# Starting four first-MLP sums of the first batch before their last third is there

## The chip, the cores and the metric

One core of a Trainium2 chip runs the whole program. The metric is device microseconds of one execution; the number given for a kernel is the median over its runs. Engines are called PE (TensorE matmul; PEld its weight loads), ACT (ScalarE), DVE (VectorE), POOL (GpSimd) and SP (SyncE, which issues most DMAs).

## What is computed

Attention with normalised queries and keys over 8 batches, 12 heads, 448 positions, 64 channels, and then one MLP over the 3584 tokens that come out:

```python
q_n, k_n = rmsnorm(q, g_q), rmsnorm(k, g_k)
attn = softmax(q_n @ k_n.T / 8)            # per batch and head
x = (attn @ v) -> (3584 tokens, 768)       # heads side by side
h = x @ w_in                               # 768 -> 2048
g = max(h, 0) + alpha * min(h, 0)          # alpha: one number per column
out = g @ w_out                            # 2048 -> 768
```

## The kernel before

**Tiles.** A batch's 12 heads are cut in three groups of four (G = 3), so there are 24 groups, numbered y = 3 b + i. A group has seven score tiles (y, j), one per 64 keys: `score` (L212) makes one with four matmuls (line 217) into one of two PSUM tiles `sc` of two banks each (pool `pss`, L55), and `soft` (L226) takes its exponential on ACT into `expT` (line 229). When all seven are there, `den` (L249) sums them over the keys with 28 matmuls against ones (line 240, tile `dn`), `log` and `invert` (L253, L258) turn that into 1/sum on ACT as exp(-ln), and `attv` (L262) makes the 28 matmuls with v (line 240, tile `av`) and lets DVE multiply both into the group's third of `xT[b]` (line 268). `dn`, `av`, the transposes `tps2` of groups 3 to 7, and some MLP tiles (`hTa`, `opa`) all use the one PSUM tile of pool `psa`, tag "acc" (two banks, one buffer); the other MLP tiles rotate through two banks of `psf`, tag "mm". Together they are eight banks.

**Before the scores**, each group's q and k are loaded (`load_qk`, SP's queue, six buffers `nat`), squared on POOL (`square`, line 135), summed on DVE (`reduce`, line 141), turned into factors by two small ACT steps (`root`, lines 152 and 153), scaled to fp16 (`scale`, line 158, on POOL but for a few on DVE), and transposed: groups 0 to 7 on PE with two DVE copies that give qT and kT (`turn`, lines 193, 202 and 204), the later ones by DMA (`turn_dma`) with a small DVE step (line 179).

**The MLP** of a batch: 16 units "up" (L279), each six matmuls 128x128 by 128x448 over the six thirds-by-two of `xT[b]` (line 284), then ACT's scaled copy `ah` (line 292) and DVE's maximum into `gT` (line 293); the sums over 768 need all three groups of the batch, the third last. And units "down" (L297): 16 matmuls over all of `gT` and `w_out_sb` (line 301) for 128 tokens and half of the columns, a DVE copy, and the store. Two batches give 14 of them. The weights come by POOL's DMA queue in four pieces each (`load_w_in`, `load_w_out`).

**Order.** Nothing reorders: each engine does its instructions as the program emits them. The program goes through 66 "bursts" n (L489). A burst emits two or three score tiles and their exponentials, and a `den` (in `dens`), an `attv` (in `avs`) or neither ("plain"); then a root and its scalings, then the MLP units planned for it, `gaps[n]`, among which the `turn` of a coming group stands. In a plain burst whose first unit is an up, the second exponential waits behind that unit's `ah` ("late", L518). The planner (L384 to L440) gives units costs of 1.13 and 2.6, cuts the run into periods that begin with the `attv` of a batch's third group, and fills each burst until a clock passes its share. `prep` and `post` hold loads, squares and reduces by burst; `jobs` holds reduces that follow the burst's units or go inside its first down. Two bursts are `lead` (L494): the `den` of group 2 (burst 11) and its `attv` (burst 12) go before the scores there, and in 11 eight and in 12 three matmuls on zeros (`spin`, L323) keep PE busy.

Of the kernel before, what the change touches and what calls it, by code (L numbers as in the profile page):

```python
# [9 lines left out]
FP32 = mybir.dt.float32  # L10
# [11 lines left out]
def kernel(  # L22
# [12 lines left out]
    nc = tc.nc  # L35

    B, H, S, D = q.shape
# [4 lines left out]
    G = HH // 2  # L42
# [188 lines left out]
            scale=QK_SCALE, bias=expb[:, 0:1],  # L231
        )

    def over_keys(name, y, weights):
        acc = psa.tile([128, 2, 512], FP32, name=name, tag="acc")
        e = expT[y]
        for j in range(J):
            for g in range(2):
                for par in range(2):
                    nc.tensor.matmul(  # L240
                        out=acc[ds(64 * par, 64), g, :S],
                        lhsT=weights(g, par, j),
                        rhs=e[ds(64 * g, 64), j, par, :],
                        start=(j == 0),
                        stop=(j == J - 1),
                    )
        return acc
# [11 lines left out]
        r = rden[y]  # L259
        nc.scalar.activation(out=r, in_=r, func=AF.Exp, scale=-1.0)  # L260

    def attv(y):  # L262
        b, i = divmod(y, G)
        vv = vt[b]
        av = over_keys("av", y, lambda g, par, j: vv[ds(64 * g, 64), 2 * i + par, j, :])
        if i == 0:
            xT[b] = att.tile([128, 2, G, S], FP16, name="xT", tag="xT")
        nc.vector.tensor_mul(  # L268
            out=xT[b][:, :, i, :], in0=av[:, :, :S], in1=rden[y]
        )  # L270


    def bank(name, spare):
        if spare:
            t = psa.tile([128, 2, 512], FP32, name=name + "a", tag="acc")
            return t[:, 0]
        return psf.tile([128, 512], FP32, name=name, tag="mm")

    def up(b, ft, spare=False):  # L279
        x = xT[b].rearrange("p g i c -> p (g i) c")  # L280
        hT = bank("hT", spare)
        order = [g * G + i for i in range(G) for g in range(2)]
        for c in order:
            nc.tensor.matmul(  # L284
                out=hT[:, :S],
                lhsT=w_in_sb[:, c, ts(ft, 128)],
                rhs=x[:, c, :],
                start=(c == order[0]),
                stop=(c == order[-1]),
            )  # L290
        ah = ffn.tile([128, S], FP16, name="ah", tag="ah", bufs=3)
        nc.scalar.activation(out=ah, in_=hT[:, :S], func=AF.Copy, scale=alpha_sb[:, ft : ft + 1])  # L292
        nc.vector.tensor_max(out=gT[:, ft, ds((b & 1) * S, S)], in0=hT[:, :S], in1=ah)  # L293
# [43 lines left out]
    while m < NG * J or len(avs) < NG:  # L337
        n = len(bursts)
        if len(dens) > len(avs):
            avs[n] = len(avs)  # L340
        elif len(dens) < NG and last_in.get(len(dens), n) < n:
            dens[n] = len(dens)
        three = n in dens and dens[n] >= G or n in avs and avs[n] >= G
        count = min(3 if three else 2, NG * J - m)
        bursts.append([divmod(m + c, J) for c in range(count)])
        for y, j in bursts[n]:
            first_in.setdefault(y, n)
            if j == J - 1:
                last_in[y] = n
        m += count  # L350
# [5 lines left out]
    def at(n, f, *a):  # L356
        prep.setdefault(max(int(n), 0), []).append((f, a))
# [4 lines left out]
    turn_at = {  # L362
        y: max(n for n in range(first_in[y]) if n not in dens) for y in range(1, NG)
    }
    turn_at[2] = av_at[0] + 1
    turns = {n: y for y, n in turn_at.items()}
    jobs = {}
    for y in range(G, NG):

        early = y < G + 2  # L370
        n = turn_at[y - 1] if early else max(d for d in dens if d <= turn_at[y] - 2)
        at(n - (8 if early else 5), load_qk, y)
        for nm in "qk":
            (after if early else at)(n - 2, square, y, nm)
            if early:
                after(n, reduce, y, nm)
            else:
                jobs.setdefault(n, []).append((reduce, (y, nm)))
        roots[n + 1] = y
    for b in range(1, B):  # L380
        at(av_at[G * b] - 4, load_v, b)


    UP, DOWN = 1.13, 2.6  # L384

    periods, carry = [], []
    for b in range(B):
        ups = [(UP, up, (b, ft)) for ft in range(NF)]
        odd = b % 2
        new = [  # L390
            (DOWN, down, (b - odd, t, oh))
            for t in (range(3, J) if odd else range(3)) for oh in range(2)
        ]
        tail = len(new) if b == B - 1 else 2 if odd or b == 0 else 1
        periods.append((ups, carry, new[:tail]))
        carry = new[tail:]

# [11 lines left out]
    for b in range(B - 1):  # L409
        lo, hi = av_at[G * b + G - 1], av_at[G * b + 2 * G - 1]  # L410
        ups, old, new = (list(u) for u in periods[b])
        mlp = sum(u[0] for u in ups + old + new)
        per = (mlp + sum(cost(n) for n in range(lo, hi))) / (hi - lo)
        clock = 0.0
        for n in range(lo, hi):
            clock += cost(n)
            free = True
            while ups or old or new:
                if old and (not ups or free and (
                    wide(n) or len(old) > sum(wide(c) for c in range(n, hi))  # L420
                )):
                    u = old.pop(0)
                elif ups:
                    u = ups.pop(0)
                else:
                    u = new.pop(0)
                gaps[n].append(u[1:])
                clock += u[0]
                free = False
                ahead = 0.5 * (UP if ups else DOWN)  # L430
                short = n in turns and len(gaps[n]) < 2
                if n < hi - 1 and not short and clock + ahead > per * (n - lo + 1):
                    break
# [55 lines left out]
    for n in range(NB):  # L489
        for f, a in prep.get(n, ()):  # L490
            f(*a)
        tiles = bursts[n]

        lead = n in (den_at[G - 1], av_at[G - 1])  # L494
        if lead and n in dens:
            den(dens[n])
            log(dens[n])
            invert(dens[n])
        elif lead:
            attv(avs[n])  # L500
        for t in tiles[:2]:
            score(*t)
        plain = n not in dens and n not in avs
        wait = plain and gaps[n] and gaps[n][0][0] is up
        if lead and n in avs:
            spin(3)
        for t in tiles[:1] if wait else tiles[:2]:
            soft(*t)
        if n in dens and not lead:
            den(dens[n])  # L510
        if n in avs and not lead:
            attv(avs[n])
        for t in tiles[2:]:
            score(*t)
            soft(*t)
        late = []
        if wait:
            late = [(1, soft, t) for t in tiles[1:]]  # L518
        if n in roots:
            y = roots[n]  # L520
            root(y)
            for nm in "qk":
                scale(y, nm)
            if y >= TD:
                turn_dma(y)
        if n in dens and not lead:
            log(dens[n])
            if gaps[n] and gaps[n][0][0] is down:
                invert(dens[n])
            else:  # L530
                late = [(1, invert, (dens[n],))]
        done = 0

        spare_at, clock = [], 0.0
        for k, (f, a) in enumerate(gaps[n][:-1]):
            free = 2.3 if n in dens else 1.2 if n in avs else 0.1
            if clock >= free and not turns.get(n, TD) < TD and (
                not spare_at or k - spare_at[-1] > 2
            ):
                spare_at.append(k)  # L540
            clock += DOWN if f is down else UP
        for k, (f, a) in enumerate(gaps[n]):
            spare = k in spare_at
            if f is down:
                down(*a, jobs.pop(n, ()), spare)
            else:
                f(*a, spare)
                done += 1
                if late and done == late[0][0]:
                    for _, g, c in late:  # L550
                        g(*c)
                    late = []
            if n in turns and k == (
                0 if turns[n] >= TD else max(min(1, len(gaps[n]) - 2), 0)
            ):
                turn(turns[n])
        if not gaps[n] and n in turns:
            turn(turns[n])
        for _, g, c in late:
            g(*c)  # L560
        if n < den_at[G - 1] - 1 and plain and n not in turns:
            spin(4)
        elif lead and n in dens:
            spin(8)
        for f, a in jobs.pop(n, []) + post.get(n, []):
            f(*a)
    for k, (f, a) in enumerate(rest):
# [31 lines left out]
```

## Time and profile before

| | |
|---|---|
| median of 13 runs | 449.79 us (449.39 to 450.77) |
| the profiled execution | 450.65 us, of which the span of the trace is 448.8 us |
| busy in the span: PE, PEld, ACT, DVE, POOL | 425.9, 230.4, 290.6, 207.7, 171.2 us |
| matmuls of "up" (line 284) | 353 ns each as shown, 12 in a row start every 0.19 us |
| exponential of a score tile (line 229) | 1007 ns as shown, 0.90 us from one to the next in a row |
| `ah`, `gT` (lines 292, 293) | 634 and 624 ns |

PE's matmuls overlap, so what an instruction costs in a row is the distance between starts, not its own length; ACT's and DVE's overlap a little too.

The bursts can be found in PE's timeline by their score matmuls (line 217). Before: burst 10 starts at 38.23 us, 14 at 56.32, 15 at 60.71, 16 at 67.95, 17 at 73.16, 18 at 77.55, 19 at 86.64, 20 at 89.03, 21 at 97.55, 24 at 115.60, 26 at 127.81.

### The profile page before, as it was taken

The page shows a single profiled execution, that of the slowest core. Times are in us where ns is not written, and L with a number is a line of the kernel's source. Part 1 is how long each engine was busy: PE and PEld are TensorE (multiplying, and loading weights), DVE is VectorE, ACT ScalarE, POOL GpSimd, SP SyncE. Part 2 cuts the span into 40 slices and gives each one's busy share as a digit, 9 for nine tenths or more (in the row PEclk, how much of TensorE's full clock was granted, in tenths as well). Part 3 has the DMA queues.
Part 4 walks back from the last instruction along what each step waited for, and adds up shares of the span by engine and source line. Part 5 has one row for each costly group of instructions (what it writes and reads, how often), then busy time and mean ns, then how long its engine had stood idle before and what let it go on. Part 6 is the DMA issues. An engine that isn't in the chain of part 4 may idle for free.

```text
span 448.8 us, 9101 instructions
## 1 busy us (share of the span) xinstructions
PE 425.9 (95%) x3844; PEld 230.4 (51%) x3844; DVE 207.7 (46%) x297; ACT 290.6 (65%) x401; POOL 171.2 (38%) x125
## 2 busy tenths in 40 slices
PE   6867889899999999999999999999999999999996
PEld 3344444555545555545555545545555555555563
DVE  3656454735454545445453545444553343243421
ACT  4899788578675868568675868568775857222300
POOL 5769954660671460760671460760542000000000
PEclk9799999999999999999999999999999999999999
DMA  8999997295656651872666651772353401111122
GB/s 189 228 236 242 231 242 144 32 182 127 144 96 140 160 121 38 124 179 79 142 101 172 159 125 37 137 176 69 77 95 79 77 2 37 37 35 37 35 72 70
DMA packets 60009, 52.77 MB, mean 118 GB/s; under 512 B 32688, under 2 KB 56512, under 8 KB 59968
## 3 DMA queue, kind: packets, MB, share of 16 engines
q1 hardware_dynamic: 47424, 39.27, 37.3%
q0 software_dynamic: 11808, 11.81, 16.8%
q10 hardware_dynamic: 736, 1.11, 1.0%
q8 instruction: 30, 0.49, 0.5%
q14 instruction: 11, 0.09, 0.1%
HBM read 45.62 MB, written 11.01 MB: 126 GB/s over the span
## 4 chain that ended last, share of the span: by engine, by line
PE 82%; ACT 10%; DVE 4%; DMA 1%; issue 1%; POOL 0%; SPq 0%; ACTq 0%
PE op L301 32%; PE hT L284 19%; PE hTa L284 10%; PE sc L217 8%; ACT expT L229 6%; PE dn L240 5%; PE av L240 5%; PE opa L301 2%; PE tps L193 1%; ACT ah L292 1%; DMA nat<-in_k_dram 1%; ACT rden L260 1%; ACT rden L255 1%; DVE gT L293 1%; DVE ss L141 1%
## 5 line engine op out<-in xcount | busy, mean ns | idle before, releaser
L229 ACT ACTIVATE expT<-sc,expb 128x896 f16<-128x896 f32 x168 | 158.2, 1007 | 20.0 <-PE sc L217 19.7
L301 PE MATMUL op<-w_out_sb,gT 128*128 128x384 f16 x848 | 145.4, 326 | 0.0
L158 POOL TENSOR_TENSOR qs<-nat,rr 128x896 f16<-128x896 f32 x44 | 78.3, 1799 | 175.0 <-issue 138.2
L301 PEld LDWEIGHTS <-gT 128*128 128x128 f16 x896 | 84.6, 98 | 62.4 <-issue 9.1
L284 PE MATMUL hT<-xT,w_in_sb 128*128 128x448 f16 x534 | 112.7, 353 | 1.4 <-DVE gT L293 1.4
L284 PEld LDWEIGHTS <-w_in_sb 128*128 128x128 f16 x768 | 73.8, 98 | 71.5 <-issue 6.8
L292 ACT ACTIVATE ah<-hT,cols 128x448 f16<-128x448 f32 x89 | 56.4, 634 | 64.4 <-PE hT L284 64.3
L293 DVE TENSOR_TENSOR gT<-hT,ah 128x448 f16<-128x448 f32 x89 | 55.5, 624 | 64.8 <-ACT ah L292 64.8
L135 POOL TENSOR_TENSOR sq<-nat 128x896 f32<-128x896 f32 x44 | 73.0, 1680 | 1.9 <-DMA nat<-in_q_dram 1.9
L313 DVE COPY osb<-op 128x384 f32<-128x384 f32 x53 | 29.5, 558 | 93.7 <-PE op L301 93.7
L217 PE MATMUL sc<-qT,kT 64*64 64x448 f16 x672 | 53.8, 364 | 9.8 <-ACT expT L229 5.1
L141 DVE TENSOR_REDUCE ss<-sq 128x14 f32<-128x896 f32 x48 | 49.9, 1076 | 6.5 <-ACT sq L133 6.3
L284 PE MATMUL hTa<-xT,w_in_sb 128*128 128x448 f16 x234 | 50.6, 352 | 0.0
L292 ACT ACTIVATE ah<-hTa,cols 128x448 f16<-128x448 f32 x39 | 24.7, 633 | 39.6 <-PE hTa L284 39.6
L293 DVE TENSOR_TENSOR gT<-hTa,ah 128x448 f16<-128x448 f32 x39 | 24.3, 624 | 34.5 <-ACT ah L292 34.5
L217 PEld LDWEIGHTS <-kT 64*64 64x64 f16 x672 | 19.1, 105 | 40.0 <-issue 28.0
L240 PE MATMUL av<-expT,vt 64*64 64x448 f16 x672 | 36.0, 350 | 2.2 <-ACT rden L255 2.2
L240 PE MATMUL dn<-expT,ones 64*64 64x448 f16 x672 | 35.9, 349 | 0.2 <-DVE gT L293 0.2
L268 DVE TENSOR_TENSOR xT<-av,rden 128x896 f16<-128x896 f32 x24 | 26.2, 1091 | 21.3 <-PE av L240 20.2
L240 PEld LDWEIGHTS <-vt 64*64 64x64 f16 x672 | 20.6, 107 | 14.0 <-issue 3.7
L240 PEld LDWEIGHTS <-ones 64*64 64x64 f16 x672 | 20.6, 107 | 11.5 <-issue 0.6
L260 ACT ACTIVATE rden<-rden 128x896 f32<-128x896 f32 x24 | 22.9, 953 | 0.7
(37 smaller groups left out, 132.8 us busy)
## 6 DMA issues: line engine op xcount, KB each, us to landing
out_dram<-osb SPq DMA_DIRECT2D x54, 192.0 KB, 2.7
nat<-in_q_dram SPq DMA_DIRECT2D x46, 224.0 KB, 6.3
nat<-in_k_dram SPq DMA_DIRECT2D x46, 224.0 KB, 7.1
vt<-in_v_dram POOLq DMA_DIRECT2D x16, 336.0 KB, 8.3
w_in_sb<-in_moe_w_in_dram POOLq DMA_DIRECT2D x4, 768.0 KB, 12.7
w_out_sb<-in_moe_w_out_dram POOLq DMA_DIRECT2D x4, 768.0 KB, 16.4
nat<-in_q_dram ACTq DMA_DIRECT2D x2, 224.0 KB, 5.0
nat<-in_k_dram ACTq DMA_DIRECT2D x2, 224.0 KB, 6.7
```

The costliest lines, as they stand in the source:

```text
L135: nc.gpsimd.tensor_mul(out=sqf, in0=src, in1=src)
L141: nc.vector.tensor_reduce(out=ss_t[y][:, "qk".index(nm)].rearrange("p h j -> p (h j)").unsqueeze(2), in_=sqs[y, nm], axis=AXIS_X, op=ALU.add,)
L158: eng.tensor_mul(out=t.rearrange("p j h d -> p h j d"), in0=nat[y, nm], in1=rr_t[y][:, "qk".index(nm)].unsqueeze(3).broadcast_to((128, 2, ...
L217: nc.tensor.matmul(out=sc[ds(64 * g, 64), par, :S].rearrange("p (j c) -> p j c", j=J), lhsT=kT[ds(64 * par, 64), j, g, :], rhs=qT[ds(64 * ...
L229: nc.scalar.activation(out=expT[y][:, j], in_=scs[y, j][:, :, :S], func=AF.Exp, scale=QK_SCALE, bias=expb[:, 0:1],)
L240: nc.tensor.matmul(out=acc[ds(64 * par, 64), g, :S], lhsT=weights(g, par, j), rhs=e[ds(64 * g, 64), j, par, :], start=(j == 0), stop=(j == ...
L260: nc.scalar.activation(out=r, in_=r, func=AF.Exp, scale=-1.0)
L284: nc.tensor.matmul(out=hT[:, :S], lhsT=w_in_sb[:, c, ts(ft, 128)], rhs=x[:, c, :], start=(c == order[0]), stop=(c == order[-1]),)
L292: nc.scalar.activation(out=ah, in_=hT[:, :S], func=AF.Copy, scale=alpha_sb[:, ft : ft + 1])
L293: nc.vector.tensor_max(out=gT[:, ft, ds((b & 1) * S, S)], in0=hT[:, :S], in1=ah)
L301: nc.tensor.matmul(out=op[:, :OH], lhsT=gT[:, ft, ts(t, 128)], rhs=w_out_sb[:, ft, ds(oh * OH, OH)], start=(ft == 0), stop=(ft == NF - 1),)
L313: nc.vector.tensor_copy(out=o[:, ds(oh * OH, OH)], in_=op[:, :OH])
```

## The change

1. Group 2's `den` and `attv` both stand in burst 11 (`avs` gets the same n). Its `av` goes into a score tile of `pss` instead of "acc"; `log` and `invert` are emitted after the av matmuls and ahead of the exponentials and of group 4's root.
2. The first four up units of batch 0 (ft 0 to 3) are split (`up_part`, `begin`): four matmuls each over groups 0 and 1, held in PSUM, and two each over group 2 later. Unit 0 begins in burst 10 between its two scores (a bank of `psf`), 1 and 2 between the two scores of burst 11, 3 after them; 2 and 3 share the "acc" tile, one bank each, and are ended together before the `ah` of 2. The other up units are as before; the same matmuls are summed in the same order.
3. The eleven zero matmuls of bursts 11 and 12 are gone. Burst 6 gets four (it is now plain and without a turn).
4. The turn of group 2 is in burst 5, not 6; that of group 4 comes after the first unit of burst 13, not the second; group 4's root and scalings in burst 11, not 10.
5. v is loaded six bursts ahead of a batch's first `attv`, not four; `w_out` comes one burst earlier (9 to 12).
6. In a burst whose first unit is an up, `jobs` (bursts 11, 14 and 24) and a DVE step of `turn` (burst 25) go ahead of the units.
7. The planner counts the four begun units a third, starts batch 0's period a burst earlier, keeps three downs in it instead of two, and spreads last downs one to a burst.

The planner's loops, followed by hand, give these units (u = up, d = down, with the number of them); up to burst 10 there are none, and from burst 28 on the two plans are the same:

| burst | 11 | 12 | 13 | 14 | 15 | 16 | 17 | 18 | 19 | 20 | 21 | 22 | 23 | 24 | 25 | 26 | 27 |
|---|---|---|---|---|---|---|---|---|---|---|---|---|---|---|---|---|---|
| before | - | 3u | 3u | 2u | 2u | 4u | 2u | 2d | - | d u | 4u | d u | d 2u | d u | 3u | 4u | 2d |
| after | 5u | 3u | 3u | 2u | 2u | u | d | d | d | d u | 4u | d u | d u | 3u | 3u | 3u d | d |

```diff
@@ -231,8 +231,9 @@
             scale=QK_SCALE, bias=expb[:, 0:1],
         )
 
-    def over_keys(name, y, weights):
-        acc = psa.tile([128, 2, 512], FP32, name=name, tag="acc")
+    def over_keys(name, y, weights, spare=False):
+        pool, tag = (pss, "sc") if spare else (psa, "acc")
+        acc = pool.tile([128, 2, 512], FP32, name=name, tag=tag)
         e = expT[y]
         for j in range(J):
             for g in range(2):
@@ -259,10 +260,14 @@
         r = rden[y]
         nc.scalar.activation(out=r, in_=r, func=AF.Exp, scale=-1.0)
 
-    def attv(y):
+    def attv(y, spare=False, jobs=()):
         b, i = divmod(y, G)
         vv = vt[b]
-        av = over_keys("av", y, lambda g, par, j: vv[ds(64 * g, 64), 2 * i + par, j, :])
+        av = over_keys(
+            "av", y, lambda g, par, j: vv[ds(64 * g, 64), 2 * i + par, j, :], spare
+        )
+        for f in jobs:
+            f(y)
         if i == 0:
             xT[b] = att.tile([128, 2, G, S], FP16, name="xT", tag="xT")
         nc.vector.tensor_mul(
@@ -276,18 +281,38 @@
             return t[:, 0]
         return psf.tile([128, 512], FP32, name=name, tag="mm")
 
+    begun = {}
+
+    def up_part(hT, b, ft, lo, hi):
+
+        for i in range(lo, hi):
+            for g in range(2):
+                nc.tensor.matmul(
+                    out=hT[:, :S],
+                    lhsT=w_in_sb[:, g * G + i, ts(ft, 128)],
+                    rhs=xT[b][:, g, i, :],
+                    start=(i == 0 and g == 0),
+                    stop=(i == G - 1 and g == 1),
+                )
+
+    def begin(ft):
+
+        if ft < 2:
+            begun[ft] = bank("hT", False)
+        elif ft == 2:
+            t = psa.tile([128, 2, 512], FP32, name="hTb", tag="acc")
+            begun[2], begun[3] = t[:, 0], t[:, 1]
+        up_part(begun[ft], 0, ft, 0, G - 1)
+
     def up(b, ft, spare=False):
-        x = xT[b].rearrange("p g i c -> p (g i) c")
-        hT = bank("hT", spare)
-        order = [g * G + i for i in range(G) for g in range(2)]
-        for c in order:
-            nc.tensor.matmul(
-                out=hT[:, :S],
-                lhsT=w_in_sb[:, c, ts(ft, 128)],
-                rhs=x[:, c, :],
-                start=(c == order[0]),
-                stop=(c == order[-1]),
-            )
+        if b == 0 and ft in begun:
+            hT = begun[ft]
+
+            for n in {2: (2, 3), 3: ()}.get(ft, (ft,)):
+                up_part(begun[n], 0, n, G - 1, G)
+        else:
+            hT = bank("hT", spare)
+            up_part(hT, b, ft, 0, G)
         ah = ffn.tile([128, S], FP16, name="ah", tag="ah", bufs=3)
         nc.scalar.activation(out=ah, in_=hT[:, :S], func=AF.Copy, scale=alpha_sb[:, ft : ft + 1])
         nc.vector.tensor_max(out=gT[:, ft, ds((b & 1) * S, S)], in0=hT[:, :S], in1=ah)
@@ -340,6 +365,8 @@
             avs[n] = len(avs)
         elif len(dens) < NG and last_in.get(len(dens), n) < n:
             dens[n] = len(dens)
+            if dens[n] == G - 1:
+                avs[n] = G - 1
         three = n in dens and dens[n] >= G or n in avs and avs[n] >= G
         count = min(3 if three else 2, NG * J - m)
         bursts.append([divmod(m + c, J) for c in range(count)])
@@ -362,13 +389,13 @@
     turn_at = {
         y: max(n for n in range(first_in[y]) if n not in dens) for y in range(1, NG)
     }
-    turn_at[2] = av_at[0] + 1
+    turn_at[2] = av_at[0]
     turns = {n: y for y, n in turn_at.items()}
     jobs = {}
     for y in range(G, NG):
 
         early = y < G + 2
-        n = turn_at[y - 1] if early else max(d for d in dens if d <= turn_at[y] - 2)
+        n = turn_at[y - 1] + (y == G) if early else max(d for d in dens if d <= turn_at[y] - 2)
         at(n - (8 if early else 5), load_qk, y)
         for nm in "qk":
             (after if early else at)(n - 2, square, y, nm)
@@ -376,22 +403,22 @@
                 after(n, reduce, y, nm)
             else:
                 jobs.setdefault(n, []).append((reduce, (y, nm)))
-        roots[n + 1] = y
+        roots[n + 1 + (y == G + 1)] = y
     for b in range(1, B):
-        at(av_at[G * b] - 4, load_v, b)
+        at(av_at[G * b] - 6, load_v, b)
 
 
     UP, DOWN = 1.13, 2.6
 
     periods, carry = [], []
     for b in range(B):
-        ups = [(UP, up, (b, ft)) for ft in range(NF)]
+        ups = [(UP / 3 if b == 0 and ft < 4 else UP, up, (b, ft)) for ft in range(NF)]
         odd = b % 2
         new = [
             (DOWN, down, (b - odd, t, oh))
             for t in (range(3, J) if odd else range(3)) for oh in range(2)
         ]
-        tail = len(new) if b == B - 1 else 2 if odd or b == 0 else 1
+        tail = len(new) if b == B - 1 else 3 if b == 0 else 2 if odd else 1
         periods.append((ups, carry, new[:tail]))
         carry = new[tail:]
 
@@ -428,6 +455,8 @@
                 clock += u[0]
                 free = False
                 ahead = 0.5 * (UP if ups else DOWN)
+                if not (ups or old) and n + len(new) < hi:
+                    break
                 short = n in turns and len(gaps[n]) < 2
                 if n < hi - 1 and not short and clock + ahead > per * (n - lo + 1):
                     break
@@ -491,19 +520,21 @@
             f(*a)
         tiles = bursts[n]
 
-        lead = n in (den_at[G - 1], av_at[G - 1])
-        if lead and n in dens:
+        lead = n == den_at[G - 1]
+        if lead:
             den(dens[n])
-            log(dens[n])
-            invert(dens[n])
-        elif lead:
-            attv(avs[n])
+            attv(avs[n], True, (log, invert))
         for t in tiles[:2]:
             score(*t)
-        plain = n not in dens and n not in avs
-        wait = plain and gaps[n] and gaps[n][0][0] is up
-        if lead and n in avs:
-            spin(3)
+            if lead and t == tiles[0]:
+                begin(1)
+                begin(2)
+            elif n == den_at[G - 1] - 1 and t == tiles[0]:
+                begin(0)
+        plain = lead or n not in dens and n not in avs
+        wait = plain and not lead and gaps[n] and gaps[n][0][0] is up
+        if lead:
+            begin(3)
         for t in tiles[:1] if wait else tiles[:2]:
             soft(*t)
         if n in dens and not lead:
@@ -539,6 +570,13 @@
             ):
                 spare_at.append(k)
             clock += DOWN if f is down else UP
+        ups_first = gaps[n] and gaps[n][0][0] is up
+        if ups_first:
+            for f, a in jobs.pop(n, ()):
+                f(*a)
+        turned = n in turns and turns[n] >= TD and ups_first
+        if turned:
+            turn(turns[n])
         for k, (f, a) in enumerate(gaps[n]):
             spare = k in spare_at
             if f is down:
@@ -550,8 +588,8 @@
                     for _, g, c in late:
                         g(*c)
                     late = []
-            if n in turns and k == (
-                0 if turns[n] >= TD else max(min(1, len(gaps[n]) - 2), 0)
+            if n in turns and not turned and k == (
+                0 if turns[n] >= TD or plain else max(min(1, len(gaps[n]) - 2), 0)
             ):
                 turn(turns[n])
         if not gaps[n] and n in turns:
@@ -560,8 +598,6 @@
             g(*c)
         if n < den_at[G - 1] - 1 and plain and n not in turns:
             spin(4)
-        elif lead and n in dens:
-            spin(8)
         for f, a in jobs.pop(n, []) + post.get(n, []):
             f(*a)
     for k, (f, a) in enumerate(rest):
```

## The prediction, as put on record before the run

> **What bounds the kernel now.** I read the slices of the page first, then PE's waits in two stretches, then PE's and ACT's timelines around bursts 10 to 12. The slices (11.2 us each):
>
> ```profile
> PE   6867889899999999999999999999999999999996
> ACT  4899788578675868568675868568775857222300
> PEclk9799999999999999999999999999999999999999
> ```
>
> PE is full from the seventh slice on; before it, it is not. PE's waits from 26 to 97 us, and then from 97 to 448:
>
> ```profile
> PE sc L217 <- ACT expT L229: 5.1, 11, 0.8
> PE sc L217 <- DVE kT L204: 2.8, 3, 1.0
> PE av L240 <- ACT rden L255: 1.3, 2, 0.9
> PE tps L193 <- DVE xT L268: 1.1, 1, 1.1
> PE hT L284 <- DVE gT L293: 0.2, 1, 0.2
> ...
> PE hT L284 <- DVE gT L293: 1.2, 3, 0.7
> PE dn L240 <- DVE gT L293: 0.2, 1, 0.2
> ```
>
> The columns are total, times, longest. So 10.5 us of waiting lie in 26 to 97, and 1.4 in the 351 us after that: from burst 21 on PE sets the time. What is moved off PE's path before 97 us, and doesn't come back, shortens the whole. The place of the change, in PE's timeline:
>
> ```profile
> 39.61 0.38 PE L217 MATMUL sc<-qT,kT 64*64 64x448 f16 x4 [0.99 <-DVE kT L204]
> 39.82 1.49 PE L240 MATMUL dn<-expT,ones 64*64 64x448 f16 x28
> 41.15 0.55 PE L217 MATMUL sc<-qT,kT 64*64 64x448 f16 x8
> 41.63 1.69 PE L328 MATMUL spin<-idle,ident 128*128 128x448 f16 x8
> 43.24 1.52 PE L240 MATMUL av<-expT,vt 64*64 64x448 f16 x28
> 44.89 0.38 PE L217 MATMUL sc<-qT,kT 64*64 64x448 f16 x4
> 45.78 0.38 PE L217 MATMUL sc<-qT,kT 64*64 64x448 f16 x4 [0.51 <-ACT expT L229]
> 46.10 0.74 PE L328 MATMUL spin<-idle,ident 128*128 128x448 f16 x3
> 46.68 2.43 PE L284 MATMUL hT<-xT,w_in_sb 128*128 128x448 f16 x12
> ```
>
> and in ACT's:
>
> ```profile
> 41.57 0.32 ACT L152 ACTIVATE rr<-ss,epsb 128x28 f32<-128x28 f32 x1 [0.52 <-DVE ss L141]
> 42.06 0.90 ACT L255 ACTIVATE rden<-dn 128x896 f32<-128x896 f32 x1
> 42.99 0.95 ACT L260 ACTIVATE rden<-rden 128x896 f32<-128x896 f32 x1
> ```
>
> The spins do no work: eleven at 0.19 are 2.06 us, counted busy. The `log` of group 2 starts 0.75 us after its `den` ended (41.31), because the root of group 4 stands ahead of it and waits for its sums. With the spins, 12.6 us are to be won in 26 to 97 at most.
>
> **What the Trainium skill says.** "Perfetto Trace Analysis", Identifying the Most-Contended Engine: busy matmul time is no good measure of the distance to the peak. The trace agrees in its way: spins count as busy. I therefore go by waits and starts. "PSUM — Partial Sum Buffer", The four PSUM rules: two open sums in one bank would clear each other's flags; in different banks they don't. Each begun unit has a bank of its own; no sum of the kernel before is left open across other matmuls, so no run yet shows this. The same page, Engine vs sequencer instructions: matmuls start and complete in program order. So a matmul that waits holds all behind it; the trace agrees (the transposes at 65.95 waited 1.1, and the up unit behind them, whose inputs were long there, starts at 66.72). "TensorE: Matmul & The Clock Gate", What's actually happening: an idle window of some 3.4 us halves the clock. PE's longest wait after 26 us is 1.12 and its clock stays at 9 tenths or more, so the spins of bursts 11 and 12 can go.
>
> **Step 1, turn of group 2 in burst 5.** Before: transposes at 28.73, kT written at 30.54, score (2,0) at 30.60, exponential at 31.03; ACT idle 0.88. After: `av` of group 0 ends at 27.15, scaled k is ready at 27.46 (POOL, 24.86 + 2.60), transposes to 28.05, DVE's xT to 28.36, then two copies at 0.62 to 29.6. The score then waits for nothing but ACT's exponentials 1.3 to 1.6, which end at 30.35 (the third starts 0.2 later than now, behind the transposes). Gain 0.7. Four new spins of burst 6 (0.75) run from 29.0 to 29.75 while ACT has work to 30.35: nothing; without that cover 0.15. This stretch is ACT's chain, so the 0.7 goes through to score (3,0), at 38.9. The root of group 3 then needs its sums by 32.1; they are there at 31.85. Ends: 0.3 if that fails, 0.9.
>
> **Step 2, bursts 10 to 13.** PE: begin(0), four matmuls at 0.19 = 0.76, fits in the 0.99 before score (3,0) (the first piece of `w_in` landed at 29.4: issue 19.1 plus 10.3). Then `den` 39.1 to 40.5, `av` at once in a score tile to 41.9, score (3,1) 42.3, begin(1) 43.1, begin(2) 43.9 ("acc" is free at `log`'s end, 41.5), score (3,2), begin(3) to 45.0. ACT: `log` 40.65, `invert` to 42.4, DVE's xT to 43.5. That added wait, score (3,2) for the tile that `av` holds, ends at 43.5, before PE comes to it; behind it would be begin(3) and all units. Their last two matmuls each: 45.0 to 46.55. Unit 4 needs a bank that gT of unit 0 frees: ACT does exponential (3,2) to 45.2, root to 45.75, `ah` to 46.4, gT 47.05, so 0.5 of waiting. Then unit 4 to 48.2; burst 12 to 52.35 (2 scores 0.7, three units 3.4); burst 13 with the turn's 0.78 to 57.1. The reduces of group 5, now ahead of gT, run 43.5 to 45.6 while DVE would wait anyway; uncovered they'd cost up to 2.0. Moved past in POOL's queue: v (1.38) and three `w_out` issues (0.8 each) now stand ahead of the scaling of group 4, which is ready at 49.0 for a turn at 53.5: 4.5 of slack.
> The sum: before, score (4,0) at 56.32 with six units done; after, 57.1 with eleven. Five units at 1.14 are 5.7, less 0.8: **4.9 ahead**, step 1 in it. Ends 3.4 (half of my closeness to ACT's chain fails) and 5.7.
>
> **Step 3, bursts 14 to 20.** Here units are missing, and ACT decides. Before: 56.32 to 97.55 = 41.2 us. Removed: five ups (5.7), added one down (16 at 0.163 = 2.6): PE's work is 3.1 less. Walking through ACT's order (0.90 per exponential, 0.81 `log`, 0.95 `invert`, 0.55 root, 0.53 to 0.63 `ah`) I find four waits: score (4,5) 0.6 on an exponential, score (5,0) 1.1 on kT (unit 13's gT and two copies stand before it), score (5,2) 1.15, since the exponential of (5,0) stands behind the only unit of burst 16, and score (6,0) 1.1 on kT, since no second down covers the turn in burst 18. They sum to 3.95; before, the same stretch had 0.59, 1.12, 0.79 and 1.6 (burst 19 with no unit), 4.1 with small ones. The reduces of group 6 go ahead of the units and so the 1.12 on DVE's xT goes; it comes back as the wait on kT. Allowing 0.4 for steps between engines, these bursts take 38.4 us: 2.8 less for 3.1 less work. **4.6 ahead** at burst 21. Ends: minus 2 and plus 2 on this.
> `w_out`: the first down begins at 73.9 and needs the fourth piece after twelve matmuls, at 75.8. It is issued near 52.5; the four pieces took
>
> ```profile
> DMA to landing us min/median/max: 11.0/16.4/17.4
> ```
>
> so 70 with the longest. Before it landed at 73.6 with the DMA engines full; the bytes ahead are the same: nothing.
>
> **Step 4, bursts 21 to 27.** In burst 24 the third unit waits for a bank: `log` and `invert` stand between its `ah`s: 0.65. Burst 25 has this now (0.67) and keeps 0.4. Cost 0.4; ends 0 and 1.2. Loads of v two bursts earlier for all batches: POOL is 38% busy; their 1.4 us stand ahead of squares and scalings needed two bursts later: nothing; without cover 1.4 once. The DVE step in burst 25 depends on a transpose issued two bursts before: nothing. From burst 28 nothing differs.
>
> **Sum.** 4.9 - 0.3 - 0.4 = 4.2. Of the profiled execution: 450.65 - 4.2 = 446.45, span 444.6. It stood 0.86 over the median; from the median 449.79 I get **445.6**.
>
> **Rivals.**
> (a) *The waits of bursts 14 to 20 mostly vanish* (2 us of step 3's upper end): 443.6. For: I took latencies in full. Against: kT's path is in the trace at 0.87 and 0.99.
> (b) *All is handed back before burst 20*: the units pulled forward leave bursts 15 to 19 as bare as burst 19 is now, which lost 1.6. Three more such bursts lose 4.8: 450.4, no change. For: ACT has 25 us of work in 14 to 19 against PE's 27.5. Against: one down of 2.6 stands in each of 17 to 19.
> (c) *Slower: `w_out` comes late.* PE then stands at the first down's thirteenth matmul, with all behind it. Each us after 75.8 costs one; the change is slower by over 0.9 from a landing at 80.9. At 30 us from issue, 82.5: 6.7 - 4.2 = 2.5 slower, 452.3. For: v and `w_out` are now nearer together while the DMA engines are full to 68. Against: the landing of today, 73.6, would do.
> (d) *The change doesn't do what it says*: begin(1) to (3) wait for the whole of xT. Then PE idles 42.3 to 43.5: 1.2 lost, 446.8. Against: `up` reads the first piece of `w_in_sb` at 46.68 while the fourth lands at 47.8, so parts of a tile are told apart.
>
> **Chances.** Forecast with (d), 443.9 to 447.5: 0.67. (a): 0.10. Partly handed back, 447.5 to 448.9: 0.08. (b), 448.9 to 450.7: 0.08. (c) and its like: 0.07. A measurement can tell about 0.2%, 0.9 us, from no change. So faster 0.85, same 0.08, slower 0.07. The range 443.3 to 448.9 leaves out 0.05 below and 0.15 above.
>
> **What would show it.** Score (3,0) near 38.9; no PE wait over 0.6 from 39 to 57; eleven up units before score (4,0) at 57; waits on kT of 1 us at groups 5 and 6; burst 21 at 95 to 96 with one down more; PE's waits after that 1.4 to 2. A wait of the first down on `w_out`, PE waits of 8 us in 57 to 95, or a clock under 0.99 would prove me wrong.

## The result, and the profile after

| | median | ratio to the kernel before |
|---|---|---|
| before | 449.77 us (32 runs) | |
| changed | 445.3 us (444.91 to 446.31, 7 runs) | 0.9897, 95% interval 0.9888 to 0.9906 |

4.5 us faster; the forecast was 445.6. The profiled execution took 445.36 us, its span 443.6.

The slices of the changed kernel's page (11.1 us each):

```profile
PE   7879998899999999999999999999999999999996
ACT  4998888667967676766875776767875767222300
PEclk9899999999999999999999999999999999999999
```

PE is full from the fourth slice on, but has two eights (67 to 89 us), where three of the waits of bursts 16 to 19 lie. PE's waits, first from 26 to 93 us (up to the start of burst 21), then from 93 to 448; the columns are total, times, longest:

```profile
PE sc L217 <- ACT expT L229: 3.2, 5, 1.3
PE sc L217 <- DVE kT L204: 2.0, 2, 1.3
PE av L241 <- ACT rden L256: 0.9, 1, 0.9
PE hT L290 <- DVE gT L318: 0.4, 1, 0.4
PE spin L353 <- DVE qT L202: 0.2, 1, 0.2
...
PE hT L290 <- DVE gT L318: 2.0, 4, 0.8
PE dn L241 <- DVE gT L318: 0.2, 1, 0.2
```

The early waits went from 10.5 to 6.7, the spins in that stretch from eleven to four, and the late waits rose from 1.4 to 2.2. PE's timeline through bursts 10 and 11, up to unit 4:

```profile
36.97 0.93 PE L290 MATMUL hT<-xT,w_in_sb 128*128 128x448 f16 x4
38.03 0.38 PE L217 MATMUL sc<-qT,kT 64*64 64x448 f16 x4
38.25 1.49 PE L241 MATMUL dn<-expT,ones 64*64 64x448 f16 x28
39.57 1.49 PE L241 MATMUL av<-expT,vt 64*64 64x448 f16 x28
40.90 0.36 PE L217 MATMUL sc<-qT,kT 64*64 64x448 f16 x4
41.19 0.93 PE L290 MATMUL hT<-xT,w_in_sb 128*128 128x448 f16 x4
41.95 0.92 PE L290 MATMUL hTb<-xT,w_in_sb 128*128 128x448 f16 x4
42.87 0.38 PE L217 MATMUL sc<-qT,kT 64*64 64x448 f16 x4
43.19 0.93 PE L290 MATMUL hTb<-xT,w_in_sb 128*128 128x448 f16 x4
43.95 0.92 PE L290 MATMUL hT<-xT,w_in_sb 128*128 128x448 f16 x4
44.71 0.92 PE L290 MATMUL hTb<-xT,w_in_sb 128*128 128x448 f16 x4
46.00 1.29 PE L290 MATMUL hT<-xT,w_in_sb 128*128 128x448 f16 x6 [0.37 <-DVE gT L318]
```

From 36.97 to 45.6 PE hardly waits. The begun sums are 16 matmuls of line 290 in four pieces of 0.76: the first, at 36.97, fills the wait for kT, the next two, at 41.19 and 41.95, the wait for xT. The fourth, at 43.19, stands behind score (3,2), which needs the tile that `av` holds until xT is done, and fills no wait. The eight matmuls at 43.95 and 44.71 end all four. ACT in the same place:

```profile
39.79 0.92 ACT L256 ACTIVATE rden<-dn 128x896 f32<-128x896 f32 x1 [0.32 <-PE dn L241]
40.74 0.95 ACT L261 ACTIVATE rden<-rden 128x896 f32<-128x896 f32 x1
...
47.05 0.63 ACT L317 ACTIVATE ah<-hTb,cols 128x448 f16<-128x448 f32 x1 [0.70 <-DVE gT L318]
```

`log` follows `den` at once. The last line I had not foreseen: the `ah` of unit 3 waits 0.70 for the gT of unit 2, in the other bank of the same tile.

Where the time came from, in the two traces. The profiled executions differ by 0.8 us before the first edit takes effect (the scaling of group 2's k starts at 24.86 us before and at 24.08 after). Of that, 0.27 is there when ACT starts to square group 0's k, for whose landing it waits (7.64 against 7.37). The rest has arisen by the first exponential, at 14.15 and 13.37; from 10.6 to 14.2 us PE's clock was 0.54 in the one and 0.84 in the other. The table takes the 0.78 off.

| place | before | after (plus 0.78) | ahead |
|---|---|---|---|
| score (3,0) | 39.61 | 38.81 | 0.8 |
| score (4,0), 6 and 11 ups done | 56.32 | 56.82 | 5.7 - 0.5 = 5.2 |
| burst 21, one down more done | 97.55 | 94.48 | 3.07 + 2.61 = 5.7 |
| burst 28, same work done | 140.28 | 135.78 | 4.5 |

"Ahead" counts the work that is done in excess: five ups (5.7) at score (4,0), one down (2.61) at burst 21. From burst 28 nothing changes: 4.5 there, 4.5 between the medians.

### The profile page after: what moved, and what is told of

Same layout as the page of the kernel before. It is cut to its first block, busy times and chain, and to the rows that moved or that the text cites. A ratio compares the mean times of both kernels' runs of the same rounds, so it can differ in the third digit from the quotient of the medians.

```text
span 443.6 us, 9091 instructions
## 1 busy us (share of the span) xinstructions
PE 424.4 (96%) x3837; PEld 228.7 (52%) x3837; DVE 206.8 (47%) x297; ACT 290.3 (65%) x401; POOL 170.8 (39%) x125
## 4 chain that ended last, share of the span: by engine, by line
PE 85%; ACT 8%; DVE 4%; DMA 1%; issue 1%; ACTq 0%
PE op L326 32%; PE hT L290 19%; PE hTa L290 10%; PE sc L217 8%; PE av L241 6%; PE dn L241 6%; ACT expT L229 5%; PE opa L326 2%; ACT ah L317 2%; DMA nat<-in_k_dram 1%; PE tps L193 1%; DVE gT L318 1%; ACT rden L256 1%; DVE kT L204 1%; PE spin L353 1%; DVE qT L202 1%
## 5 line engine op out<-in xcount | busy, mean ns | idle before, releaser
L290 PE MATMUL hTa<-xT,w_in_sb 128*128 128x448 f16 x228 | 49.3, 352 | 0.0
L241 PEld LDWEIGHTS <-ones 64*64 64x64 f16 x672 | 20.9, 107 | 11.1 <-issue 0.6
## 6 DMA issues: line engine op xcount, KB each, us to landing
w_in_sb<-in_moe_w_in_dram POOLq DMA_DIRECT2D x4, 768.0 KB, 14.2
```

The lines of the kernel that those rows point to most:

```text
L241: nc.tensor.matmul(out=acc[ds(64 * par, 64), g, :S], lhsT=weights(g, par, j), rhs=e[ds(64 * g, 64), j, par, :], start=(j == 0), stop=(j == ...
L290: nc.tensor.matmul(out=hT[:, :S], lhsT=w_in_sb[:, g * G + i, ts(ft, 128)], rhs=xT[b][:, g, i, :], start=(i == 0 and g == 0), stop=(i == G ...
```

## The experiments

All were timed in five rounds against the kernel before; "changed" is the kernel above, at 445.3 us. The edits are to the changed kernel unless it is said otherwise, and three dots in a diff stand for lines left out.

The kernel before had medians of 449.8 to 450.4 us in these rounds, so a difference of some tenths between medians of two rounds says little. The traces allow a finer comparison. From ACT's `log` of group 0 to the start of PE's last two downs, the kernel before takes 414.44 us and the changed one 409.94, which is the 4.50 again. "Lined up" is the same distance in another trace, less 409.94; each is one execution.

**The begun thirds.** This kernel leaves nothing out; the four units are whole.

```diff
-            if lead and t == tiles[0]:
-                begin(1)
-                begin(2)
-            elif n == den_at[G - 1] - 1 and t == tiles[0]:
-                begin(0)
...
-        if lead:
-            begin(3)
```

> The changed kernel, but up units 0 to 3 of batch 0 are not begun: all six matmuls of each stand after group 2's xT, and the den and attv of group 2 stay together in burst 11. Theory (the begun thirds fill time in which PE would stand waiting for log, invert and xT): PE waits for xT from about 41.2 to 42.8 instead of working, and 16 matmuls at 0.19 = 3.0 us stand after it; less 0.4, the wait of unit 4 on a bank, which falls away: 2.6 us slower than the changed kernel, 448.0. Rival (the gain is that of the joined den and attv, of log ahead of the root and of the spins left out; the thirds only move work within a stretch that ACT paces): at most 0.5 slower, 445.3 to 445.8.

447.68 us (447.41 to 448.64), ratio 0.9947 (0.993 to 0.9964): 2.4 slower than the changed kernel; lined up, 2.29. PE's timeline:

```profile
40.97 0.36 PE L217 MATMUL sc<-qT,kT 64*64 64x448 f16 x4
42.94 0.38 PE L217 MATMUL sc<-qT,kT 64*64 64x448 f16 x4 [1.62 <-DVE xT L273]
43.26 2.44 PE L290 MATMUL hT<-xT,w_in_sb 128*128 128x448 f16 x12
```

PE stands 1.62 for xT, and the wait for kT at score (3,0) is back at 1.00. So the begun sums filled waits, as the theory has it, and its rival is out. Its two terms were not right, though: not 16 matmuls are lost but the 12 that had stood in waits (12 at 0.19 are 2.28), for the fourth piece fills none; and unit 4's wait on a bank, 0.37, does not fall away.

Some 2.1 of the 4.5 are therefore not the begun thirds'. This trace also shows where the head start comes from: counted from `log` of group 0, score (3,0) is 0.79 ahead of the kernel before (14.14 for 14.93) and the first up 2.71 (19.29 for 22.00). The difference, 1.9, is what the joined `den` and `attv`, with `log` ahead of the root, give; no run takes these two apart (the spins, left out at the same place, gain nothing by the run further down). With the 2.3 of the begun sums this makes 5.0, of the 5.2 at score (4,0); later bursts give some back.

**The turn of group 2.**

```diff
-    turn_at[2] = av_at[0]
+    turn_at[2] = av_at[0] + 1
...
-        n = turn_at[y - 1] + (y == G) if early else max(d for d in dens if d <= turn_at[y] - 2)
+        n = turn_at[y - 1] if early else max(d for d in dens if d <= turn_at[y] - 2)
```

> The changed kernel with group 2's turn back in burst 6; group 3's squares, sums and root stay where they are; the four spins of burst 6 go, since it has a turn again. Theory (ACT stood idle 0.88 until kT of group 2 was there, and nothing after that gives the time back): 0.8 slower, 446.1; in the trace score (2,0) and all behind it 0.8 later. Rival (PE and ACT have slack between 30 and 57, so that a later start is caught up with): 0.2 slower at most.

446.35 us (445.76 to 446.48), ratio 0.9912 (0.9894 to 0.993): 1.05 slower; lined up, 0.83. ACT's timeline has the wait of the kernel before back:

```profile
30.42 1.91 ACT L229 ACTIVATE expT<-sc,expb 128x896 f16<-128x896 f32 x2 [0.88 <-PE sc L217]
```

Counted from ACT's `log` of group 0 (24.07 here, 23.90 in the changed kernel), score (2,0) at 29.98 is 0.80 later than 29.01. So 0.8 is step 1's, kept to the end.

**Ending units 2 and 3 apart.**

```diff
-            for n in {2: (2, 3), 3: ()}.get(ft, (ft,)):
-                up_part(begun[n], 0, n, G - 1, G)
+            up_part(hT, 0, ft, G - 1, G)
```

> The changed kernel, but units 2 and 3, which share one PSUM tile in two banks, are ended one after the other: two matmuls of 2, its ah and gT, and only then two matmuls of 3. Theory (in the trace of the changed kernel the ah of unit 3 starts only when gT of unit 2 has ended, though the two are in different banks, so accesses of different engines to one tile are put in order): the two matmuls of unit 3 wait for gT of unit 2, until about 47.0 instead of 45.3, unit 4 behind them starts at 47.4 instead of 46.0, and of the 1.4 a part is made up by waits behind it that fall away: 0.9 slower (0.3 to 1.4), 446.2. Rival (banks are told apart): no change within 0.2.

446.67 us (446.53 to 446.9), ratio 0.9923 (0.9906 to 0.994): 1.4 slower, the upper end of what was expected; lined up, 1.44.

```profile
44.44 0.54 PE L290 MATMUL hTb<-xT,w_in_sb 128*128 128x448 f16 x2
46.80 0.54 PE L290 MATMUL hTb<-xT,w_in_sb 128*128 128x448 f16 x2 [1.81 <-DVE gT L317]
```

The second pair writes another bank than the first, and yet waits for the gT that reads the first. The program orders the engines by tile here, not by bank. Ending them together keeps that wait off PE; only ACT has it (the 0.70 above). Parts of `xT`, on the other hand, are told apart: begin(1) runs at 41.19, before group 2's third is written. Why this PSUM tile is not treated so, no run shows.

**The spins alone**, in the kernel before:

```diff
-        if lead and n in avs:
-            spin(3)
...
-        elif lead and n in dens:
-            spin(8)
```

> The kernel before without the eleven spin matmuls of bursts 11 and 12 and with nothing else changed. Theory (they fill time in which PE would wait for log, and three of them end 0.5 before up unit 0 could not have started anyway): 0.0 to 0.4 faster than the kernel before, clock unchanged, 449.6. Rival 1 (they cost their 2.06 us): 447.7. Rival 2 (they keep the clock up): slower by up to 1.7, with a clock under 1 in the slices at 40 to 50 us.

449.94 us (449.51 to 451.16), ratio 0.9994 (0.9983 to 1.0006): no change. The 2.06 us of spins lay in waits; leaving them out gives nothing by itself. In its trace PE's clock is 0.66 at 38 to 40 us and 0.50 at 40 to 42, and this one execution, lined up with that of the kernel before, is 0.55 longer. The removed spins would have begun after 41.3, so their absence can't be the cause of a dip that starts at 38; whether they would have shortened it stays open. The prediction let the spins go because no wait of PE was longer than 1.12. By this trace that is no safe ground: the clock fell although no wait since 10 us was longer than 0.99. In the changed kernel begun sums stand in that place, and its clock there is 1.00.

**The planner's edits.**

```diff
-        tail = len(new) if b == B - 1 else 3 if b == 0 else 2 if odd else 1
+        tail = len(new) if b == B - 1 else 2 if odd or b == 0 else 1
...
-                if not (ups or old) and n + len(new) < hi:
-                    break
```

> The changed kernel with the planner's last two edits undone: two downs, not three, stay in batch 0's period, and last downs are not spread. By hand: burst 13 has two ups, 16 two, 19 nothing, 20 to 27 as in the kernel before. Theory (these edits trade waits for waits): burst 19 without a unit loses 1.6 as in the kernel before, the 1.3 of score (5,2) behind the only unit of burst 16 falls to 0.2, and the 0.85 of unit 1.9 in burst 24 falls away: 0.4 faster (0.9 faster to 0.4 slower), 444.9. Rival (a unit in every burst of 16 to 19 is what keeps the gain): 1.5 or more slower, 446.8.

445.63 us (445.44 to 446.38), ratio 0.9894 (0.9873 to 0.9914): within the interval of the changed kernel; lined up, 0.32 slower. Its trace has burst 19's waits back (0.31, 0.52, 0.42, 0.36), score (5,2) waits 0.17 instead of 1.31, and the late waits are 1.4 instead of 2.2. Waits traded for waits, as the theory has it; the 0.4 of gain in it did not show, for the trace has a wait that I left out: with one up less in burst 13, score (4,0) stands 0.59 for kT.

**The order of the reduces.**

```diff
-        if ups_first:
-            for f, a in jobs.pop(n, ()):
-                f(*a)
-        turned = n in turns and turns[n] >= TD and ups_first
+        turned = False
```

> The changed kernel with the reduces of jobs after the units again in bursts 11, 14 and 24, and the DVE step of the turn in burst 25 after the first unit. Theory: the transposes of group 5 wait about 1.1 for xT of group 3 behind the reduces of group 6, as in the kernel before, and the 0.7 that score (5,0) waits for kT becomes less or stays, since kT is then later too: 0.5 slower (0 to 0.9), 445.8. Rival 1: all of 1.1 is lost, 446.4. Rival 2: faster, since gT no longer stands behind sums, 444.9.

447.36 us (447.02 to 448.18), ratio 0.993 (0.9911 to 0.995): 2.1 slower, more than the theory and both rivals gave; lined up, 2.03. Most of the cause is in burst 12, where I had not looked. ACT's timeline, then PE's:

```profile
50.52 0.32 ACT L152 ACTIVATE rr<-ss,epsb 128x28 f32<-128x28 f32 x1 [1.78 <-DVE ss L141]
```

```profile
52.56 0.38 PE L217 MATMUL sc<-qT,kT 64*64 64x448 f16 x4 [1.31 <-ACT expT L229]
```

The sums of group 5 now stand behind five gT on DVE, the root waits 1.78 for them, the exponential of (3,4) and the `ah`s stand behind the root, and score (3,6) waits 1.31 on that. To tell this from burst 14's share, a run with burst 11 alone:

```diff
-        if ups_first:
+        if ups_first and not lead:
             for f, a in jobs.pop(n, ()):
```

> The changed kernel with the reduces of group 5 behind the units of burst 11 again, those of bursts 14 and 24 and the step in burst 25 left ahead. New theory for the 2.0 us of the run with all of them late: the root of group 5, in front of which nothing may pass on ACT, waits 1.8 for sums that stand behind five gT, the exponential of (3,4) comes later by that and score (3,6) waits 1.3; the reduces of burst 14 account for the other 0.4: 1.5 slower than the changed kernel (1.1 to 1.8), 446.8. Rival (burst 14 accounts for most of it, 1.1 or more): 0.9 slower or less.

446.65 us (446.57 to 446.76), ratio 0.9916 (0.9901 to 0.9931): 1.35 slower; lined up, 1.53; the same 1.31 in the trace, and the waits of bursts 14 to 16 as in the changed kernel. So about 1.5 is burst 11's, and 0.5 the rest's: in the run with all late the transposes of group 5 wait 1.12 for xT, score (5,0) no longer waits its 0.71, and the wait in burst 25 is 0.77 instead of 0.67.

**The loads.**

```diff
-        at(av_at[G * b] - 6, load_v, b)
+        at(av_at[G * b] - 4, load_v, b)
...
-        at(first - 2 + c, load_w_out, c)
+        at(first - 1 + c, load_w_out, c)
```

> The changed kernel with v loaded four bursts ahead and the pieces of w_out in bursts 10 to 13, as in the kernel before. Theory (the loads have slack): the fourth piece is issued near 55.6 and lands near 74 with 18 to 19 us, the first down needs it at 74.7: 0 to 0.3 slower, 445.4. Rival (the earlier loads are part of the gain): 1 or more slower, with the first down waiting in the middle.

445.43 us (445.1 to 446.11), ratio 0.9889 (0.987 to 0.9908): the same; lined up, 0.00. The last piece was issued at 56.0 and took 19.1 us, so it landed at 75.1, and the first down, which begins at 73.27 here and needs the piece after twelve matmuls, at 75.2, does not pause. So it arrived with 0.1 to spare. The earlier issue gains nothing, but it is the margin: in the changed kernel it is 3.9 us.

**The waits that were left**, to see whether they cost what they say. First the exponential that stands behind burst 16's only unit:

```diff
-        wait = plain and not lead and gaps[n] and gaps[n][0][0] is up
+        wait = plain and not lead and len(gaps[n]) > 1 and gaps[n][0][0] is up
```

> The changed kernel with the second exponential of a plain burst held back behind the first unit only if the burst has two units or more; that touches burst 16 alone. Theory (score (5,2) waits 1.31 for the exponential of (5,0), which stands behind the only unit of the burst): the exponential of (5,0) starts at 68.2 and not 69.9, score (5,2) waits for nothing, ah of unit 15 comes 0.3 later, which the first down covers, and since PE sets the end the time goes through: 1.1 faster (0.6 to 1.3), 444.2. Rival (the wait moves to den of group 4, or to the next exponential): no change within 0.3.

443.72 us (443.65 to 444.14), ratio 0.9851 (0.9831 to 0.9871): 1.6 faster than the changed kernel, more than the 0.6 to 1.3 expected; lined up, 1.50. Scores (5,1) and (5,2) now follow one another:

```profile
69.08 0.57 PE L217 MATMUL sc<-qT,kT 64*64 64x448 f16 x8
```

Then the turn of group 6 in the middle of burst 18's only down, whose sum stays open in its bank meanwhile:

```diff
...
+            if mid is not None and ft == 7:
+                turn(mid)
...
-                down(*a, jobs.pop(n, ()), spare)
+                mid = turns[n] if len(gaps[n]) == 1 and turns.get(n, TD) < TD else None
+                down(*a, jobs.pop(n, ()), spare, mid)
+                if mid is not None:
+                    continue
```

> The changed kernel with the turn of group 6 inside the only down unit of burst 18, after its eighth matmul, instead of behind it; the down's sum stays open in its bank meanwhile. Theory (score (6,0) waits 1.31 for kT, because nothing on PE covers DVE's two copies): the eight matmuls behind the transposes (1.3 us) cover them, the wait falls to 0.1, and PE sets the end: 1.2 faster than the changed kernel (0.8 to 1.3), 444.1. Rival (the transposes must wait for xT of group 4, which holds the tile, or the next wait takes over): less than 0.4 faster.

443.93 us (443.75 to 444.2), ratio 0.9854 (0.9838 to 0.9871): 1.4 faster; lined up, 1.27. Both edits:

> The changed kernel with the second exponential of burst 16 not held back and the turn of group 6 inside the down. Theory (two separate waits of PE ahead of a stretch that PE sets): the gains add up, 1.6 + 1.2 = 2.8 faster than the changed kernel, 442.5. Rival (ACT sets the pace of bursts 14 to 19 and hands back half): 443.5 or more.

442.62 us (442.23 to 443.61), ratio 0.983 (0.9814 to 0.9845): 2.7 faster; lined up, 2.78, and 1.50 and 1.27 are 2.77. They add up. Last, `log` behind the first `ah`:

```diff
+            if gaps[n] and gaps[n][0][0] is up:
+                late = [(1, log, (dens[n],)), (1, invert, (dens[n],))]
...
```

> As the last, and in a burst with a den whose first unit is an up (14 and 24) log goes behind the first unit's ah instead of ahead of it. Theory (unit 1.9 of batch 1 waits 0.85 in burst 24 for a bank, because log and invert stand between the ahs of the units before it): ah of the first unit comes 0.8 earlier, the wait falls to 0.1, attv still finds its tile free: 0.7 faster than with two edits (0.4 to 0.85), 441.8. Rival (attv then waits for log): no gain.

442.12 us (442.03 to 443.09), ratio 0.982 (0.9806 to 0.9835): the best run, 3.2 faster than the changed kernel, 0.5 of it by this edit (by the medians; the intervals of the two overlap). Lined up it is 3.03, so only 0.25 by this edit, less than expected: the wait of unit 1.9 falls by 0.60, but small delays elsewhere, at `av` and the score behind it in bursts 15 and 25, hand back about half. PE's timeline of this kernel at burst 18 and in burst 24:

```profile
75.96 1.47 PE L326 MATMUL op<-w_out_sb,gT 128*128 128x384 f16 x8
77.27 0.94 PE L193 MATMUL tps<-ident,qs 128*128 128x128 f16 x14
78.05 1.46 PE L326 MATMUL op<-w_out_sb,gT 128*128 128x384 f16 x8
79.52 0.57 PE L217 MATMUL sc<-qT,kT 64*64 64x448 f16 x8
...
112.68 1.29 PE L290 MATMUL hT<-xT,w_in_sb 128*128 128x448 f16 x6 [0.25 <-DVE gT L318]
```

Score (6,0) follows the half down without a wait, and unit 1.9 (unit 9 of batch 1) waits 0.25 instead of 0.85.

## Why the prediction was right, step by step

**PE sets the end from 97 us on.** Right. Waits put in or taken out ahead of that came out at the end: in the runs with one such wait a listed 1.31 made 1.35, 1.6 and 1.4 (lined up 1.53, 1.50 and 1.27).

**Step 1, 0.7.** 0.80 in the trace, and 1.05 when undone, in an interval that holds 0.8 (lined up, 0.83).

**Step 2, 4.9 ahead at burst 14.** 5.2. `log`'s place, xT's, the wait of unit 4 (0.37 for 0.5) and the begun sums in the waits are as worked out, but that the fourth of them fills no wait; begin(1) runs at 41.19, before xT of group 2 is written (41.72), so rival (d) is out. What I passed over is the `ah` of unit 3 behind gT of unit 2, which PE doesn't feel, and what the reduces' place is for: I priced its harm, and it prevents 1.5.

**Step 3, 4.6 ahead at burst 21.** 5.7. The four waits are the ones named, in the changed kernel's PE timeline:

```profile
63.12 0.38 PE L217 MATMUL sc<-qT,kT 64*64 64x448 f16 x4 [0.79 <-ACT expT L229]
...
67.67 0.38 PE L217 MATMUL sc<-qT,kT 64*64 64x448 f16 x4 [0.71 <-DVE kT L204]
...
69.23 0.38 PE L217 MATMUL sc<-qT,kT 64*64 64x448 f16 x4
70.92 0.38 PE L217 MATMUL sc<-qT,kT 64*64 64x448 f16 x4 [1.31 <-ACT expT L229]
...
82.33 0.57 PE L217 MATMUL sc<-qT,kT 64*64 64x448 f16 x8 [1.31 <-DVE kT L204]
```

They sum to 4.12, where I had 3.95. The bursts still take 37.7 us and not 38.4. The 0.4 that I added "for steps between engines" was not needed. And what I passed over is that a wait costs PE more than the idle time listed for it, since matmuls in a row overlap and those on the two sides of a wait don't. Scores (5,1) and (5,2) start 1.69 apart; in a row, as at 56.04, two scores take 0.40, so 0.20 each. The wait took 1.49, of which 1.31 is listed; the other three took 0.16 to 0.18 more too. Before, the same bursts had seven waits:

```profile
63.20 0.38 PE L217 MATMUL sc<-qT,kT 64*64 64x448 f16 x4 [0.59 <-ACT expT L229]
...
65.95 0.94 PE L193 MATMUL tps<-ident,qs 128*128 128x128 f16 x14 [1.12 <-DVE xT L268]
...
80.24 0.38 PE L217 MATMUL sc<-qT,kT 64*64 64x448 f16 x4 [0.79 <-ACT expT L229]
...
89.03 0.38 PE L217 MATMUL sc<-qT,kT 64*64 64x448 f16 x4 [0.31 <-ACT expT L229]
89.93 0.38 PE L217 MATMUL sc<-qT,kT 64*64 64x448 f16 x4 [0.51 <-ACT expT L229]
90.73 1.52 PE L240 MATMUL av<-expT,vt 64*64 64x448 f16 x28 [0.42 <-ACT rden L255]
92.61 0.38 PE L217 MATMUL sc<-qT,kT 64*64 64x448 f16 x4 [0.36 <-ACT expT L229]
```

They list 4.10, as much as the four after, so the listed waits show no gain at all; but three waits fewer are 0.5. With the 0.4, and less the 0.2 by which the four were longer, this is the 0.7.

**Step 4, minus 0.4.** Minus 1.2, at the end of its range. The same view:

```profile
116.09 1.29 PE L290 MATMUL hT<-xT,w_in_sb 128*128 128x448 f16 x6 [0.85 <-DVE gT L318]
...
122.44 1.29 PE L290 MATMUL hT<-xT,w_in_sb 128*128 128x448 f16 x6 [0.67 <-DVE gT L318]
```

Unit 1.9 waits 0.85 and not 0.65, which costs 1.02 from start to start (by the starts of the units, as above), and burst 25 keeps its whole 0.67, from which I had taken a part off. The last 0.17 stands ahead of burst 24: with one up less in burst 23, its first score comes 1.40 after the up ahead of it (109.38 to 110.78), where 1.23 is usual, and the DVE step of its turn (line 179) ends just before it, at 110.72. That step 3 erred by 0.8 one way and step 4 by 0.8 the other is luck: with either alone, and the 0.3 of step 2, the forecast would have been off by 1.1 or 0.5.

**Signs.** Of those that the prediction named, two missed: burst 21 stands at 94.5, not at 95 to 96, and the later waits are 2.2, not 1.4 to 2. The waits on kT were 0.71 and 1.31, not 1 each.

**Rivals.** (a) did not happen, but the waits it speaks of were real: two edits took 2.7 off. (b) is refuted by burst 21, with 5.7 ahead. (d) is out by begin(1), though its argument, that parts of a tile are told apart, did not hold for the PSUM tile of units 2 and 3. (c): the fourth piece of `w_out`, issued at 51.4, took 19.4 us and landed at 70.8, 3.9 before it was needed at 74.7. The pieces took 14.1 to 23.1 us, longer than the 11.0 to 17.4 before; three of them are issued in a row, but the fourth, issued alone, was slower too, so the reason stays open. Loading later changed nothing. The sum left open in its bank across other matmuls, which no run of before showed (unit 0's is open from 36.97 to 43.95), works as the Trainium skill says ("PSUM — Partial Sum Buffer", The four PSUM rules), and works for a down in halves too.

## What to carry to other kernels

Where a matmul unit waits only for its last inputs, begin its sum early and hold it in PSUM; it is worth the part of the work that fits into waits (12 of 16 matmuls, 2.3 us here), if the bank is free and the pieces that share a tile end together. When PE sets the end, price a reordering on every queue: the place of two sums on DVE behind five other steps cost 1.5 us through a 0.3 us step on ACT. Count the waits as well as summing them: here each cost about 0.17 us more than was listed. After such a change, the waits named in the trace of the short bursts can be taken one by one; the first two added up, the third gave half.

## What the runs showed of the hardware

The clock of PE between 10 and 20 us differs from one execution to the next: its mean was 0.66 in the profile of before, 0.83 in that of the changed kernel and of two others, and 1.00 in the rest. The landing of group 0's k differs too: ACT begins to square it at 7.26 to 7.91. The two together put `log` of group 0 at 23.54 to 24.68 us. That is more than one of the edits is worth, so two traces must be lined up behind it before their ends are compared.

In one run the clock was at half speed from 40 to 42 us, although PE had waited no longer than 0.99 us at a time since 10 us; it had been busy for 56% to 76% of each two microseconds from 34 to 40.

A wait of PE took some 0.17 us more than the idle time listed for it. That fits the overlap of matmuls in a row: one of an up is shown with 0.35, and the next starts after 0.19.
